# Linear attention with an MLP behind it: one more group with seven block products, and another order of the hand-written steps

## The chip, the cores and the metric

The kernel runs on one core of a Trainium2 chip. The metric is the device time of one launch in microseconds. A core has five engines that run side by side, each with its own queue of instructions, worked off in order: TensorE (PE: matmuls, with PEld for weight loads), VectorE (DVE), ScalarE (ACT), GpSimd (POOL) and SyncE (SP). Here SyncE issues almost all DMAs; the transfers themselves run on 16 DMA engines. An engine's instruction waits on semaphores for what it needs, and everything behind it on that engine waits with it.

## The reference

Inputs are q, k and v of shape (4, 8, 768, 64) (batch, heads, positions, features), a decay `lam` per head, a gain `g_ln` of 512, and two weights of 512 x 2048 and 2048 x 512. The attention is linear, with a decaying state, in blocks of 64 positions:

```
intra = (q_b k_b^T * Dmask) v_b            # Dmask[i,j] = lam^(i-j) for i >= j, else 0
inter = (q_b * lam^(i+1)) state
out_b = intra + inter
state = lam^64 * state + (k_b * lam^(63-i))^T v_b
```

Its output, with the heads side by side, is x of shape (4, 768, 512). Then

```
xn  = (x - mean) / sqrt(var + 1e-6) * g_ln
out = x + relu(xn @ W1) @ W2
```

All inputs and the output are float32.

## The kernel before, in words

**Windows.** The 768 positions of the four batches are cut into 12 windows of 256 positions (`u` = 0 to 11; the batch is `u % 4`). A window's attention yields two tiles of 128 positions, and these two form one *group* of the MLP, also 0 to 11. Windows 0 to 5 and windows 6 to 11 use two forms of the attention; the second has blocks of 64 (`kv64`, `scores64`, `av64`).

**Steps of a window.**
- `open_in` and `load_in` (L87, L92): input tiles `kin`, `qin`, `vin` (three buffers each) and their DMAs on SyncE (L75; from window 6 on two DMAs of 256 KB for each of k, q and v, L79).
- `in_k_one`, `in_q_one`, `in_v` (L240, L245, L251): cast or scale to bf16 in `kq` and `vb`. The engine is an argument: ScalarE, GpSimd or VectorE.
- `transpose_dma` (L266): SyncE issues DMA transposes of k (`a` = 0) and q (`a` = 1) into `kqT`.
- `s1` to `s4` for windows up to 5: `s1` does k-v products (`kv`, L316), the first half's scores (L282), states (L326 on VectorE, L322 on GpSimd) and masks (L292 on VectorE); `s2` the second half's scores and masks; `s3` attention times v (L428) and the first part of the state's share (`inter`, L441) with `seen`, a small read of its result (L452); `s4` the second part, and `norm`: ScalarE copies the result from PSUM to `x` (L463), VectorE takes mean and variance (L465, L466) and writes `xc` (L470).
- `X(u)`, or `X1` and `X2`, for windows from 6 on: the attention's end for window u - 1 (L428 or L415, L441, `norm`) together with the start for window u (L381 k-v products, L362 scores, L397 and L400 states, L368 masks).
- `to_xT` (L486): SyncE issues a DMA transpose of each half of `xc` into `xT`.
- `rstd_of` (L496, L498) and `store` (L698): the factor of the normalization, and the output's DMAs.

**The MLP of a group.** `m1` has 8 units of 8 matmuls of 128 x 256 (L530), each followed by a Relu on ScalarE into `hT` (L533). The second product has two forms, and `WG` (L45) tells from which group on the second is used:
- plain: 8 units of 4 matmuls of 128 x 512 (L666), a tile being finished on VectorE (L690);
- seven block products (`m2w`, `product`, `evict`): hidden blocks are paired, and each pair's 2 x 2 block product with W2 is made with seven products in place of eight, P1 to P7, 8 matmuls of 128 x 256 each (L565), in 8 units of 7. They need sums of hidden blocks (`h_sums`, L548 to L550, VectorE), sums of W2's blocks (`w_sums(c, n)`, L787, L788 and L790, L791, VectorE; four quarters `c`, two halves `n`), and an eviction for each product: L589 and L597 on ScalarE, L590 and L598 on GpSimd, L578 on VectorE.

**PSUM.** A pool `mm` of four banks serves `m1`, both forms of the second product and the k-v products; a new tile waits for the reader of the tile that had its bank. The seven products use all four (`pwa` to `pwd`).

**Order.** Nothing reorders the instructions: the kernel takes manual scheduling, so each engine does its work in the order in which the Python text issues it. The tail of the kernel is a long list of steps, in which `units(n)` takes the next n units of the MLP's plan (group after group, first `m1`, then the second product). A step's place in that list decides its place in the queue of every engine that it uses, SyncE's included.

Of the kernel before, what the change touches and what calls it, by code (L numbers as in the profile page):

```python
# [17 lines left out]
def kernel(  # L18
# [11 lines left out]
    nc = tc.nc  # L30
# [14 lines left out]
    WG = 6  # L45
# [216 lines left out]
    def transpose_dma(u, a):  # L262
        s = st[u]
        if "kqT" not in s:
            s["kqT"] = wk.tile([128, 2, NP, 2, 128], BF16, tag="kqT", bufs=3, name="kqT")
        nc.sync.dma_start_transpose(s["kqT"][:, a].rearrange("p b j t -> p (b j) t"),  # L266
                                    s["kq"][:, a].rearrange("p b j e d -> p (b j e d)"))
# [243 lines left out]
    m2s = {}  # L511
# [184 lines left out]
    def store(u):  # L696
        for j in range(2):
            nc.sync.dma_start(rows_of(u)[j], o_of[u][half[j]])  # L698
# [329 lines left out]
    def units(n):  # L1028
        for _ in range(n):
            f, *a = next(steps)  # L1030
            f(*a)
# [71 lines left out]
    units(2)  # L1103
    rstd_of(3)
    make_keep64()
    units(3)
    store(2)
    transpose_dma(5, 0)
    transpose_dma(5, 1)
    units(1)  # L1110
    s1(4)
    open_in(7, False)
    load_in(7, "k", nc.sync)
    units(1)
    open_window(6)
    in_k_one(6, nc.gpsimd, 0)
    in_k_one(6, nc.gpsimd, 1)
    in_q_one(6, nc.gpsimd, 0)
    in_q_one(6, nc.gpsimd, 1)
    in_v(6, nc.gpsimd)  # L1120
    units(1)
    s2(4)
    units(2)
    s3(4)
    units(2)
    s4(4)
    to_xT(4, 0)
    to_xT(4, 1)
    load_in(7, "q", nc.sync)
    units(2)  # L1130
    transpose_dma(6, 0)
    transpose_dma(6, 1)
    load_in(7, "v", nc.sync)
    units(4)
    s1(5)
    rstd_of(4)
    open_window(7)
# [3 lines left out]
    in_k_one(7, nc.scalar, 1)  # L1141
    units(1)
    s2(5)
    units(3)
    X1(6)
    in_q_one(7, nc.gpsimd, 0)
    in_q_one(7, nc.gpsimd, 1)
    units(1)
    store(3)
    units(1)  # L1150
    transpose_dma(7, 0)
    transpose_dma(7, 1)
    open_in(8, False)
    load_in(8, "k", nc.sync)
    units(2)
    X2(6)
    to_xT(5, 0)
    to_xT(5, 1)
    in_v(7, nc.gpsimd)
# [3 lines left out]
    w_sums(0, 0)  # L1163
    units(1)
    w_sums(0, 1)
    units(1)
    w_sums(1, 0)
    rstd_of(5)
    units(1)
    w_sums(1, 1)  # L1170
    units(4)
    X(7)
    store(4)
    open_in(9, False)
    load_in(9, "k", nc.sync)
    units(1)
    to_xT(6, 0)
    to_xT(6, 1)
    open_window(8)
    in_q_one(8, nc.gpsimd, 0)  # L1180
    in_q_one(8, nc.gpsimd, 1)
    units(1)
    in_k_one(8, nc.scalar, 0)
    units(1)
    in_k_one(8, nc.scalar, 1)
    transpose_dma(8, 0)
    transpose_dma(8, 1)
    load_in(9, "q", nc.sync)
    load_in(9, "v", nc.sync)
    units(2)  # L1190
    in_v(8, nc.gpsimd)
    units(2)
    rstd_of(6)
    units(2)
    w_sums(2, 0)
    units(1)
    w_sums(2, 1)
    units(1)
    w_sums(3, 0)
    units(1)  # L1200
    w_sums(3, 1)
    units(4)
    X(8)
    open_in(10, False)
    load_in(10, "k", nc.sync)
    units(1)
    to_xT(7, 0)
    to_xT(7, 1)
    open_window(9)
    in_q_one(9, nc.gpsimd, 0)  # L1210
    in_q_one(9, nc.gpsimd, 1)
    units(1)
    in_k_one(9, nc.scalar, 0)
    units(1)
    in_k_one(9, nc.scalar, 1)
    transpose_dma(9, 0)
    transpose_dma(9, 1)
    load_in(10, "q", nc.sync)
    load_in(10, "v", nc.sync)
    units(1)  # L1220
    m2s[6].sums(0, 4)
    units(1)
    in_v(9, nc.gpsimd)
    units(2)
    rstd_of(7)
    units(1)
    m2s[6].sums(4, 8)
    units(8)
    X(9)
    open_in(11, False)  # L1230
    load_in(11, "k", nc.sync)
    units(1)
    to_xT(8, 0)
    to_xT(8, 1)
    open_window(10)
    in_q_one(10, nc.gpsimd, 0)
    in_q_one(10, nc.gpsimd, 1)
    units(1)
    in_k_one(10, nc.scalar, 0)
    units(1)  # L1240
    in_k_one(10, nc.scalar, 1)
    transpose_dma(10, 0)
    transpose_dma(10, 1)
    load_in(11, "q", nc.sync)
    load_in(11, "v", nc.sync)
    units(1)
    m2s[7].sums(0, 4)
    units(1)
    in_v(10, nc.gpsimd)
    units(2)  # L1250
    rstd_of(8)
    units(1)
    m2s[7].sums(4, 8)
    units(8)
# [85 lines left out]
```

## Time and profile before

| | before |
|---|---|
| time, median of 5 runs | 213.73 us (211.63 to 215.04) |
| the profiled execution | 213.23 us, with a span of 211.5 us from first to last instruction |
| TensorE busy | 199.8 us (94%) |
| VectorE busy | 142.2 us (67%) |
| ScalarE, GpSimd busy | 97.7 us (46%), 83.0 us (39%) |
| L530, m1's matmuls | 736, 85.0 us |
| L666, plain second product | 192, 43.3 us |
| L548, L549, L550, sums of hidden blocks | 12 each, mean 0.76, 0.60, 0.59 us |

Busy times are from the profile of one execution. Matmuls are pipelined, so that a group's mean length is longer than the distance from one start to the next; where a block of matmuls is priced, starts are subtracted. A wait is put down in the profile to what ended last of what an instruction waits for. The granted TensorE clock is 0.996 of full speed.

### The profile page before, as it was taken

How to read it: one execution, taken by the hardware profiler on the slowest of the kernel's cores; microseconds unless marked ns; L12 is line 12 of the kernel's file. 1: busy time of each engine (PE TensorE's matmuls, PEld its weight loads, DVE VectorE, ACT ScalarE, POOL GpSimd, SP SyncE). 2: the span in 40 equal slices, each digit the busy share in tenths (PEclk: the TensorE clock that was granted, in tenths of full speed). 3: DMA queues.
4: the chain of work that ended last, by engine and by line, in shares of the span. 5: the costliest groups of instructions: out<-in, count | busy, mean ns of one | idle time of the engine just before them, and what ended most of it. 6: DMA issues, size and time to landing. Idle time of an engine off the chain costs nothing.

```text
span 211.5 us, 7148 instructions
## 1 busy us (share of the span) xinstructions
PE 199.8 (94%) x3079; PEld 151.6 (72%) x3079; DVE 142.2 (67%) x293; ACT 97.7 (46%) x195; POOL 83.0 (39%) x113
## 2 busy tenths in 40 slices
PE   2989999999899999999999989999999999999992
PEld 1478788544685576487487478888888888888881
DVE  2577660659267354746997789799797886876253
ACT  3855779120253145246066067185284372661630
POOL 4649039129656083208144155273192202011020
PEclk9999999999999999999999999999999999999998
DMA  4999999999999799999979799997918850430303
GB/s 111 295 271 217 209 287 158 222 299 253 154 334 219 167 224 189 190 183 214 206 170 234 136 212 180 174 213 137 205 31 163 272 141 0 105 52 0 99 16 87
DMA packets 94305, 37.17 MB, mean 176 GB/s; under 512 B 68417, under 2 KB 91457, under 8 KB 94274
## 3 DMA queue, kind: packets, MB, share of 16 engines
q1 hardware_dynamic: 89664, 32.32, 73.8%
q0 software_dynamic: 4224, 4.19, 12.5%
q8 instruction: 24, 0.39, 0.8%
q10 hardware_dynamic: 386, 0.20, 0.4%
q14 instruction: 7, 0.06, 0.1%
HBM read 27.27 MB, written 6.29 MB: 159 GB/s over the span
## 4 chain that ended last, share of the span: by engine, by line
PE 52%; DMA 16%; issue 13%; DVE 9%; POOL 3%; SPq 3%; ACT 1%; POOLq 0%; DVEq 0%; ACTq 0%
PE pm L530 28%; PE pm L666 8%; DMA w<-in_moe_w_ch_dram 4%; DMA qin<-in_q_dram 4%; DMA kin<-in_k_dram 3%; PE pwa L565 3%; DMA xT<-xc 3%; PE pwd L565 2%; PE pwc L565 2%; SPq L75 2%; DMA kqT<-kq 2%; PE po L441 1%; DVE kq L240 1%; DVE wt L790 1%; PE sc L282 1%
## 5 line engine op out<-in xcount | busy, mean ns | idle before, releaser
L530 PE MATMUL pm<-xT,w 128*128 128x256 bf16 x736 | 85.0, 273 | 1.1 <-DMA xT<-xc 1.1
L530 PEld LDWEIGHTS <-w 128*128 128x128 bf16 x736 | 70.0, 98 | 10.7 <-DMA xT<-xc 1.7
L533 ACT ACTIVATE hT<-pm 128x512 f16<-128x512 f32 x92 | 55.2, 602 | 40.9 <-PE pm L530 40.2
L666 PE MATMUL pm<-w,hT 128*128 128x512 f16 x192 | 43.3, 379 | 0.0
L666 PEld LDWEIGHTS <-hT 128*128 128x128 f16 x192 | 18.2, 98 | 20.5
L322 POOL TENSOR_TENSOR Sn<-Stmp,lam_s 128x256 bf16<-128x256 f32 x16 | 9.8, 614 | 50.6 <-DVE Stmp L400 31.9
L565 PEld LDWEIGHTS <-hs 128*128 128x128 f16 x192 | 18.8, 98 | 2.2
L470 DVE SCALAR_TENSOR_TENSOR xc<-po,mv,g_row 128x512 bf16<-128x512 f32 (+1 forms) x24 | 16.8, 705 | 1.8
L292 DVE TENSOR_TENSOR mA<-sc,keep 128x512 bf16<-128x512 f32 x20 | 13.1, 684 | 7.1 <-PE sc L282 7.1
L463 ACT COPY x<-po 128x512 f32<-128x512 f32 x18 | 9.9, 589 | 16.6 <-PE po L441 10.4
L565 PEld LDWEIGHTS <-hT 128*128 128x128 f16 x144 | 13.6, 98 | 2.7 <-ACT hT L533 1.2
L590 POOL TENSOR_TENSOR o<-ev_u,x 128x256 f32<-128x256 f32 x4 | 3.1, 782 | 31.5 <-ACT ev_u L589 31.5
L465 DVE BATCH_NORM_STATS2 stats<-x 128x6 f32<-128x512 f32 x18 | 12.4, 687 | 4.0 <-ACT x L463 3.9
L251 POOL TENSOR_TENSOR vb<-vin,lam_p 128x1024 bf16<-128x1024 f32 x6 | 11.4, 1899 | 6.1 <-DMA vin<-in_v_dram 6.0
L548 DVE TENSOR_TENSOR hs<-hT 128x1024 f16<-128x1024 f16 x12 | 9.1, 762 | 6.8 <-ACT hT L533 6.7
L245 POOL TENSOR_TENSOR kq<-qin,lam_q 128x512 bf16<-128x512 f32 x10 | 10.3, 1046 | 6.9 <-DMA qin<-in_q_dram 6.9
L251 POOL TENSOR_TENSOR vb<-vin,lam_v 128x1024 bf16<-128x1024 f32 (+1 forms) x7 | 11.8, 1687 | 2.7 <-DMA vin<-in_v_dram 1.7
L245 POOL TENSOR_TENSOR kq<-qin,lam_p 128x512 bf16<-128x512 f32 x12 | 12.3, 1044 | 0.7 <-DMA qin<-in_q_dram 0.7
L690 DVE SCALAR_TENSOR_TENSOR o<-pm,rstd,x 128x512 f32<-128x512 f32 x12 | 8.8, 745 | 5.2 <-PE pm L666 5.1
L368 DVE TENSOR_TENSOR mA<-sc,keep 128x512 bf16<-128x512 f32 x12 | 8.2, 683 | 1.6 <-PE sc L362 1.6
L452 ACT COPY seen<-po 128x8 f32<-128x8 f32 x8 | 1.0, 167 | 17.5 <-PE po L441 17.5
L441 PE MATMUL po<-Sn,kqT 64*64 64x64 bf16 x216 | 7.5, 198 | 0.3 <-DVE seen L452 0.3
(139 smaller groups left out, 267.7 us busy)
## 6 DMA issues: line engine op xcount, KB each, us to landing
out_dram<-o SPq DMA_DIRECT2D x18, 256.0 KB, 4.9
w<-in_moe_w_ch_dram POOLq DMA_DIRECT2D x8, 512.0 KB, 9.1
kin<-in_k_dram SPq DMA_DIRECT2D x14, 256.0 KB, 4.7
qin<-in_q_dram SPq DMA_DIRECT2D x14, 256.0 KB, 4.7
vin<-in_v_dram SPq DMA_DIRECT2D x14, 256.0 KB, 5.3
kin<-in_k_dram SPq DMA_DIRECT2D x5, 512.0 KB, 7.1
qin<-in_q_dram SPq DMA_DIRECT2D x5, 512.0 KB, 8.8
vin<-in_v_dram SPq DMA_DIRECT2D x5, 512.0 KB, 8.4
```

Source lines behind the costliest of these rows:

```text
L245: eng.tensor_tensor(part(1, st[u]["kq"], ALL)[:, :, :, j], src[:, :, :, j], lq[:, :, :, None].to_broadcast([128, NP, 2, D]), op=ALU.mult)
L251: eng.tensor_tensor(st[u]["vb"][:, hs], qkv_in[u]["v"][:, hs], lv.to_broadcast([128, n, 2, D]), op=ALU.mult)
L292: nc.vector.tensor_tensor(s[f"mA{hf}"][:, e], s[f"sc{hf}"][e], kp[:, None, :, :].to_broadcast([128, 2, 2, 128]), op=ALU.mult)
L322: eng.tensor_tensor(dst, src, lam_s[:, :, None].to_broadcast([128, NP, D]), op=ALU.mult)
L441: nc.tensor.matmul(s["po"][ab][half[jq], 2 * p + e, :], lhsT=qT[half[e], p, jq, half[ab]], rhs=s["S"][ab][jq][half[e], p, :], start=False, ...
L463: nc.scalar.copy(x, po)
L465: nc.vector.bn_stats(stats, po if early else x)
L470: nc.vector.scalar_tensor_tensor(xc[:, sl], in0=po[:, sl], scalar=mv[:, 0:1], in1=g_row[:, sl], op0=ALU.subtract, op1=ALU.mult)
L530: nc.tensor.matmul(pm[:, b, :], lhsT=w1[n // W2K][:, kk, (n % W2K) * 128:(n % W2K + 1) * 128], rhs=xT_of[g][:, kk, 0:N], start=(b == 0 and ...
L533: nc.scalar.activation(hT[:, u * NB:(u + 1) * NB, 0:N], pm, ACT.Relu)
L565: nc.tensor.matmul(pr[bank], lhsT=lhs(r), rhs=rhs, start=(first and r == 0), stop=(r == KB // 2 - 1), skip_group_check=True)
L666: nc.tensor.matmul(acc[i], lhsT=hT[:, kk, i * 128:(i + 1) * 128], rhs=w2[kk // W2K][:, kk % W2K, :], start=(kk == 0), stop=(kk == KB - 1))
```

## The change: what it does

`WG` goes from 6 to 5, so group 5 takes the seven products too. The sums of W2 are issued during groups 3 and 4 in place of groups 4 and 5, and the sums of group 5's hidden blocks (`m2s[5].sums`) are added. The steps of windows 4 to 11 between group 2's second product and group 8 stand in another order; some are cut up, and some casts and scalings change their engine. The list up to group 2 and from X(10) on is the same. In the diff, lines that both lists have in the same place are left out in part.

```diff
...
-    WG = 6
+    WG = 5
...
     load_in(6, "q", nc.sync)
     units(1)
     load_in(6, "v", nc.sync)
-    units(2)
+    units(1)
+    transpose_dma(5, 0)
+    units(1)
     rstd_of(3)
     make_keep64()
-    units(3)
-    store(2)
-    transpose_dma(5, 0)
     transpose_dma(5, 1)
-    units(1)
-    s1(4)
     open_in(7, False)
     load_in(7, "k", nc.sync)
     units(1)
+    s1(4)
     open_window(6)
-    in_k_one(6, nc.gpsimd, 0)
+    in_k_one(6, nc.scalar, 0)
+    units(1)
     in_k_one(6, nc.gpsimd, 1)
-    in_q_one(6, nc.gpsimd, 0)
-    in_q_one(6, nc.gpsimd, 1)
+    units(2)
+    open_window(7)
+    s2(4)
+    store(2)
+    units(2)
+    w_sums(0, 0)
+    w_sums(0, 1)
+    s3(4)
+    units(1)
+    w_sums(1, 0)
+    in_q_one(6, nc.vector, 1)
     in_v(6, nc.gpsimd)
-    units(1)
-    s2(4)
-    units(2)
-    s3(4)
-    units(2)
     s4(4)
+    in_q_one(6, nc.vector, 0)
+    units(3)
+    load_in(7, "q", nc.sync)
     to_xT(4, 0)
     to_xT(4, 1)
-    load_in(7, "q", nc.sync)
-    units(2)
+    units(1)
+    w_sums(2, 0)
+    units(1)
+    open_in(8, False)
+    units(1)
+    s1(5)
+    units(1)
+    transpose_dma(6, 1)
+    units(1)
+    rstd_of(4)
+    in_q_one(7, nc.gpsimd, 0)
+    units(1)
+    in_q_one(7, nc.gpsimd, 1)
+    s2(5)
     transpose_dma(6, 0)
-    transpose_dma(6, 1)
-    load_in(7, "v", nc.sync)
-    units(4)
-    s1(5)
-    rstd_of(4)
-    open_window(7)
-    units(1)
-    in_k_one(7, nc.scalar, 0)
-    units(1)
-    in_k_one(7, nc.scalar, 1)
-    units(1)
-    s2(5)
     units(3)
     X1(6)
-    in_q_one(7, nc.gpsimd, 0)
-    in_q_one(7, nc.gpsimd, 1)
-    units(1)
+    in_k_one(7, nc.vector, 1)
+    load_in(7, "v", nc.sync)
     store(3)
-    units(1)
+    load_in(8, "k", nc.sync)
+    in_v(7, nc.gpsimd)
+    units(1)
+    in_k_one(7, nc.scalar, 0)
+    units(1)
+    open_window(8)
+    units(2)
+    X2(6)
+    units(2)
+    w_sums(1, 1)
+    to_xT(5, 0)
     transpose_dma(7, 0)
     transpose_dma(7, 1)
-    open_in(8, False)
-    load_in(8, "k", nc.sync)
-    units(2)
-    X2(6)
-    to_xT(5, 0)
+    units(1)
+    open_in(9, False)
+    in_k_one(8, nc.vector, 1)
+    units(1)
+    in_k_one(8, nc.gpsimd, 0)
+    units(2)
     to_xT(5, 1)
-    in_v(7, nc.gpsimd)
+    units(1)
+    w_sums(3, 0)
+    units(1)
+    rstd_of(5)
+    w_sums(3, 1)
+    units(1)
+    w_sums(2, 1)
     load_in(8, "q", nc.sync)
     load_in(8, "v", nc.sync)
     units(2)
-    w_sums(0, 0)
-    units(1)
-    w_sums(0, 1)
-    units(1)
-    w_sums(1, 0)
-    rstd_of(5)
-    units(1)
-    w_sums(1, 1)
-    units(4)
     X(7)
-    store(4)
-    open_in(9, False)
-    load_in(9, "k", nc.sync)
-    units(1)
-    to_xT(6, 0)
-    to_xT(6, 1)
-    open_window(8)
+    units(1)
     in_q_one(8, nc.gpsimd, 0)
     in_q_one(8, nc.gpsimd, 1)
-    units(1)
-    in_k_one(8, nc.scalar, 0)
-    units(1)
-    in_k_one(8, nc.scalar, 1)
+    load_in(9, "k", nc.sync)
+    units(1)
+    in_v(8, nc.gpsimd)
+    units(1)
+    to_xT(6, 0)
+    transpose_dma(8, 1)
     transpose_dma(8, 0)
-    transpose_dma(8, 1)
+    to_xT(6, 1)
     load_in(9, "q", nc.sync)
     load_in(9, "v", nc.sync)
-    units(2)
-    in_v(8, nc.gpsimd)
-    units(2)
-    rstd_of(6)
-    units(2)
-    w_sums(2, 0)
-    units(1)
-    w_sums(2, 1)
-    units(1)
-    w_sums(3, 0)
-    units(1)
-    w_sums(3, 1)
-    units(4)
-    X(8)
     open_in(10, False)
     load_in(10, "k", nc.sync)
+    units(3)
+    m2s[5].sums(0, 4)
+    units(2)
+    store(4)
+    load_in(10, "v", nc.sync)
+    units(2)
+    open_window(9)
+    units(1)
+    m2s[5].sums(4, 8)
+    units(3)
+    in_k_one(9, nc.scalar, 0)
+    units(1)
+    in_k_one(9, nc.scalar, 1)
+    units(1)
+    in_q_one(9, nc.gpsimd, 0)
+    X(8)
+    units(1)
+    in_q_one(9, nc.gpsimd, 1)
+    open_window(10)
+    units(3)
+    open_in(11, False)
     units(1)
     to_xT(7, 0)
+    units(1)
+    rstd_of(7)
+    transpose_dma(9, 1)
+    transpose_dma(9, 0)
     to_xT(7, 1)
-    open_window(9)
-    in_q_one(9, nc.gpsimd, 0)
-    in_q_one(9, nc.gpsimd, 1)
-    units(1)
-    in_k_one(9, nc.scalar, 0)
-    units(1)
-    in_k_one(9, nc.scalar, 1)
-    transpose_dma(9, 0)
-    transpose_dma(9, 1)
+    rstd_of(6)
+    units(4)
+    m2s[6].sums(0, 4)
+    m2s[6].sums(4, 8)
+    units(3)
     load_in(10, "q", nc.sync)
-    load_in(10, "v", nc.sync)
-    units(1)
-    m2s[6].sums(0, 4)
-    units(1)
+    units(4)
     in_v(9, nc.gpsimd)
-    units(2)
-    rstd_of(7)
-    units(1)
-    m2s[6].sums(4, 8)
-    units(8)
+    in_k_one(10, nc.gpsimd, 1)
+    in_k_one(10, nc.gpsimd, 0)
     X(9)
-    open_in(11, False)
+    in_v(10, nc.gpsimd)
+    in_q_one(10, nc.gpsimd, 0)
+    units(1)
+    transpose_dma(10, 0)
+    units(1)
+    rstd_of(8)
+    in_q_one(10, nc.vector, 1)
+    units(1)
+    to_xT(8, 0)
+    units(2)
+    to_xT(8, 1)
+    units(1)
+    transpose_dma(10, 1)
+    units(3)
+    m2s[7].sums(0, 4)
+    m2s[7].sums(4, 8)
+    units(1)
+    load_in(11, "q", nc.sync)
+    units(1)
     load_in(11, "k", nc.sync)
-    units(1)
-    to_xT(8, 0)
-    to_xT(8, 1)
-    open_window(10)
-    in_q_one(10, nc.gpsimd, 0)
-    in_q_one(10, nc.gpsimd, 1)
-    units(1)
-    in_k_one(10, nc.scalar, 0)
-    units(1)
-    in_k_one(10, nc.scalar, 1)
-    transpose_dma(10, 0)
-    transpose_dma(10, 1)
-    load_in(11, "q", nc.sync)
+    units(2)
     load_in(11, "v", nc.sync)
-    units(1)
-    m2s[7].sums(0, 4)
-    units(1)
-    in_v(10, nc.gpsimd)
-    units(2)
-    rstd_of(8)
-    units(1)
-    m2s[7].sums(4, 8)
-    units(8)
+    units(3)
     X(10)
     units(1)
     to_xT(9, 0)
```

## The prediction, made before the run

> **What bounds the kernel now.** I read the page first: shares, then slices. Each digit of the slices is a tenth busy in a fortieth of the span (5.3 us).
>
> ```profile
> PE 199.8 (94%) x3079; PEld 151.6 (72%) x3079; DVE 142.2 (67%) x293; ACT 97.7 (46%) x195; POOL 83.0 (39%) x113
> ...
> PE   2989999999899999999999989999999999999992
> ...
> DVE  2577660659267354746997789799797886876253
> ...
> DMA  4999999999999799999979799997918850430303
> ```
>
> TensorE is full from slice 3 to 39, so a microsecond of matmul taken out there is a microsecond of time, and every new TensorE wait is paid in full. But the DMA engines are full too, up to slice 28 (148 us), and VectorE runs at eight tenths in the second half: two more resources with little to spare in the stretch that is reordered (69 to 150 us). Next the TensorE timeline, which has start, length, work and, in brackets, the idle time before and what ended it:
>
> ```profile
> 72.02 1.03 PE L530 MATMUL pm<-xT,w 128*128 128x256 bf16 x8 [0.25 <-DMA xT<-xc]
> ...
> 75.44 0.70 PE L282 MATMUL sc<-kqT 64*64 64x128 bf16 x16
> ...
> 105.52 0.45 PE L415 MATMUL po<-vb,mA 64*64 64x64 bf16 x32
> ...
> 106.98 0.19 PE L441 MATMUL po<-Sn,kqT 64*64 64x64 bf16 x1 [0.28 <-DVE seen L452]
> ...
> 107.30 7.18 PE L530 MATMUL pm<-xT,w 128*128 128x256 bf16 x64
> 114.32 7.07 PE L666 MATMUL pm<-w,hT 128*128 128x512 f16 x32
> ...
> 122.87 0.44 PE L362 MATMUL sc<-kqT 64*64 64x64 bf16 x32 [0.72 <-DMA kqT<-kq]
> ```
>
> These are all the waits of TensorE in the stretch: 0.25 us for group 3's xT, 0.28 us inside the scores of window 4 (15 of the 16 matmuls start only at 75.72, when the second mask of the first half is done), 0.28 us for VectorE's `seen`, 0.72 us for window 8's kqT. Together 1.53 us. Lastly the shares of the DMA engines over stretches of one or two groups (a share over 1 is transfers that overlap on the engines' rings):
>
> ```profile
> 72.00:89.70 17.70, 17.64 (x320) 11.48 (x320) 10.38 (x22) 7.19 (x13) 7.48 (x9) 1.00 1.24 204
> 89.70:107.30 17.60, 17.32 (x392) 12.04 (x385) 12.90 (x31) 6.01 (x11) 5.77 (x7) 1.00 1.14 194
> 107.30:123.40 16.10, 15.38 (x227) 10.46 (x218) 12.62 (x26) 7.03 (x15) 6.02 (x8) 1.00 0.87 187
> ```
>
> The last two columns are DMA share and GB/s. Up to 107 us the DMA engines have no slack: what is put ahead of a transfer in SyncE's order delays it by its own length.
>
> **What the Trainium skill says.** "TensorE: Matmul & The Clock Gate", Back-to-back issue gap, gives 262 cycles for 256 columns and 518 for 512 at 2.4 GHz, so about 109 and 216 ns. The trace agrees: 64 L530 matmuls take 7.09 us on the chain (111 ns), 32 L666 take 7.00 us from start to start (219 ns). "DMA: Bandwidth & Descriptors", Issuing engines are not separate DMA queues, says all issues run on the same 16 engines; here landings follow SyncE's order about 1.2 us per 256 KB load. "SBUF — State Buffer", Who interferes with whom, says a VectorE operation with two SBUF inputs, or a copy in a two-port mode, and a GpSimd operation that reads SBUF exclude each other for a whole instruction. The trace shows it: one L790 took 2.08 us, against 0.42, from 115.31 on, beside GpSimd's 1.90 us L251 that began at 115.21.
>
> **The change, part by part.** The sum is against the profiled execution, 213.23 us with 211.5 us of span; the median of the runs is 0.5 us above it.
>
> *Products of group 5.* Out go 32 L666 matmuls: 7.00 us. In come 56 L565: group 6's took 130.53 to 136.74, 6.21 us. TensorE: -0.79 us.
>
> *VectorE and the others in group 5.* VectorE loses two L690 (1.5 us) and gains six L548 to L550 (0.76+0.60+0.59, twice: 3.9 us) and six L578 (3.1 us), net +5.5 us; ScalarE gains two 0.47 us evictions, GpSimd two of 0.75 us. Four quarters of W2's sums only move. This work lies beside the matmuls, costing nothing as long as VectorE is not late for a bank, and I follow that below. `seen` of window 6 moves from VectorE to ScalarE (the test `u > WG`), which is idle there: the 0.28 us wait goes.
>
> *First half of window 4 (s1) three units of 0.88 earlier.* kv(4) now ends at about 70.2 us, but window 4's second kqT transpose, whose place in SyncE's queue is unchanged, landed at 70.70 us: new wait 0.55. What is queued behind it on TensorE is everything, so it is paid in full. In exchange group 3's xT (PE at 72.02) has a block more in front of it and is there: -0.25. s2(4) now comes three units after s1(4), so both masks are done: -0.28.
>
> *Window 6's preparation, taken from GpSimd.* Its first k half is now cast on ScalarE and waits there for k(6), landed at 74.1; behind it stands the Relu of group 3's first m1 tile, ready at 73.7, done by 75.4, and its bank is wanted again at 77.8: 0. Both q halves (L245; on VectorE some 0.7 us each, from L292's 0.68 for the same 512 columns; 2.6 if GpSimd's L251 locks one out) and seven pairs of W2's sums stand among VectorE's steps of windows 4 and 5. The tightest is the first: four sums of 1.6 us between the masks, over at 75.65, and `seen` of window 4, which is done at about 77.5; TensorE wants it at 77.6. A lock-out would delay xc(4) from 80.6 to 82.5 at most, still before SyncE gets to it. 0 (0 to 0.4).
>
> *Window 5's transposes before store(2).* They landed at 83.4 and 85.8; without the two stores (2 to 2.5 us) ahead, about 83.4 for the second. The scores of s1(5), now three units earlier, want it at 83.5 to 83.8. I take 0.1 (0 to 0.4).
>
> *Window 7's q loads ahead of group 4's xT.* This is the largest item. Landings are from the DMAs' semaphores in the trace. Before, the last xT landed at 89.05 and the matmuls wanted it at 89.73. Now two q loads of 1.2 to 1.5 us stand ahead: landing 91.5 to 92.1. The matmuls come later as well, by X1(6) in front of them (1.07 us) and the net of the waits above (0.12), so at 90.9. Wait 0.6 to 1.2; I take 0.9.
>
> *Window 6's transposes after it.* The set of transfers up to them is the old one, so they land at 95.57 as before. X2(6) wants them at 91.82 + 4 x 0.886 = 95.4. Wait 0.2.
>
> *Casts of windows 7 and 8 onto VectorE, window 8's k load ahead of window 7's transposes.* k(8) landed at 105.41; two transposes (2.0 us) fewer ahead make it 103.4. VectorE's L240 for window 8 waits for that, and behind it in VectorE's order stand half of the sums for W2's quarter 3, L690, a reciprocal, the other half, and the second half of quarter 2: 0.5+0.76+0.75+0.07+0.85+0.85 = 3.8 us, to 107.2. Then X(7)'s states: L397, L400, a mask, L397, 1.9 us with GpSimd's L322 beside the mask, to 109.1. That last one frees the bank of group 5's second m1 tile, which TensorE wants at 95.57 + 0.51 (X2) + 4 x 0.886 + 7 x 0.875 + 1.24 (X) + 0.875 + 0.886 = 108.8. Wait 0.3.
>
> *Window 7's and 8's transposes.* Window 7's land by 106.5 (same set as up to xT5 before, 106.52), wanted at about 106.5: 0. Window 8's q products are on GpSimd by 111.3, landing 3.3 us after issue, some 5 us before X(8): -0.72.
>
> *X(8) inside the last product, P3.* Its second kv bank waits for P6's two evictions (VectorE near 121.3 by the same counting, TensorE at 121.2), 0.1; P3's own eviction queues behind X(8)'s norm and frees the seventh m1 tile of group 6 at about 128.4 against 128.3: 0.1. Later steps of groups 6 to 8 (the sums of hidden blocks late; window 9's v and window 10's k on GpSimd behind the additions L590 and L598; SyncE's window 11 loads after window 10's transposes) leave 0.1 to 1 us of cover each by the same counting: 0 (0 to 0.8).
>
> Sum: saved 0.79+0.25+0.28+0.28+0.72 = 2.32; paid 0.55+0.1+0.9+0.2+0.3+0.2 = 2.25. Net -0.1: 213.1 for the profiled execution, 213.6 at the median.
>
> **The rivals.**
> 1. *Covered.* Transfers regroup so that xT and k(8) are in time, and only the certain 0.55 us is paid: 213.7 - 2.32 + 0.55 = 212.0. For it: rings interleave, so landing order is not strictly issue order. Against: shares of 1.24 and 1.14.
> 2. *Slower: VectorE held by its cast of k(8).* If that load lands where it did before (105.4), the bank is free at 111.1 instead of 109.1, so 2.05 us more: 215.7; a cast locked out by GpSimd's other half of the same k (L240 on VectorE ranged from 0.41 to 2.12 us) adds up to 1.6. I take 216.3. From k(8) later than 103.1 us on, each microsecond is one of time. For it: VectorE already has 12.9 of 17.6 us in that stretch and takes 5.5 us more soon after. Against: the two transposes really are behind it now.
> 3. That the products don't come out as meant can't be: 56 for 32 matmuls stand in TensorE's order.
>
> **How the numbers follow.** Forecast 0.50, own range 212.7 to 214.8 (its items' ends, and the slack of 0.1 us in three places). Covered 0.20, slower 0.30. Low end 211.8, below rival 1 by the spread of the runs; high end 216.6, so that only the worse part of the locked-out cast is left out. About 1% (2.1 us) is what a measurement tells here from no change. Faster by more than that needs nearly all of rival 1: 0.12. Slower by over 1%, past 215.9: most of rival 2 and a little of the forecast: 0.28. Same: 0.60.
>
> **What would show it.** Right: group 5's m2 6.2 us; waits of TensorE of some 0.5 us before window 4's scores and 0.5 to 1.2 us before group 4's first m1 on DMA xT; none before X(8)'s scores; a short one on VectorE's L397 in group 5. Wrong: no xT wait (rival 1), VectorE idle over 3 us before L240 (rival 2), or waits in groups 6 to 8, where I have none.

## The result, and the profile after

| | before | after |
|---|---|---|
| median of all executions | 212.69 us (80, 211.23 to 215.56) | 215.26 us (43, 212.88 to 218.68) |
| median without the slow ones | 212.53 us (71) | 214.50 us (28) |
| ratio, after to before, of these | | 1.0103, 95% interval 1.0085 to 1.0121 |
| profiled execution, span | 213.23 us, 211.5 us | 215.51 us, 213.8 us |
| TensorE, VectorE busy | 199.8, 142.2 us | 199.5, 146.6 us |

Here and below, an execution that took over 1.5 % more than the fastest of its kernel counts as slow and is left out of the medians and ratios of runs. The forecast was "no change" (213.6 us); measured is slower by 1.0 %. How much of that is the change's, the controls below tell. The slices of the page of after:

```profile
PE 199.5 (93%) x3103; PEld 154.3 (72%) x3103; DVE 146.6 (69%) x306; ACT 96.7 (45%) x195; POOL 82.8 (39%) x114
...
PE   2988699999999999898999998999999999999992
...
DVE  2586571448556688746879877789798896876253
...
DMA  4999999999999999999998799896969960430403
```

A slice is 5.3 us. In the reordered stretch TensorE now falls below 9 tenths in slices 17, 19 and 25 (from 85.5, 96.2 and 128.3 us on); before it did so in slice 24 alone. In the start, whose instructions are the same, slices 4 and 5 are emptier too. The timeline of the reordered stretch, with idle time before an instruction and its cause in brackets:

```profile
72.29 0.42 PE L282 MATMUL sc<-kqT 64*64 64x128 bf16 x16 [0.38 <-DMA kqT<-kq]
...
86.12 0.42 PE L282 MATMUL sc<-kqT 64*64 64x128 bf16 x16 [0.80 <-DMA kqT<-kq]
...
93.44 3.70 PE L530 MATMUL pm<-xT,w 128*128 128x256 bf16 x32
...
97.74 0.45 PE L362 MATMUL sc<-kqT 64*64 64x64 bf16 x32 [0.61 <-DMA kqT<-kq]
...
117.14 1.14 PE L565 MATMUL pwa<-w,hT 128*128 128x256 f16 x8
...
122.48 0.27 PE L565 MATMUL pwd<-w,hs 128*128 128x256 f16 x1
```

The first six products of group 5 take 122.48 - 117.14 = 5.34 us for 48 matmuls, so 6.23 us for 56: the 0.79 us are there. New are three waits for transposes of k and q (before the scores of windows 4, 5 and 6). Group 4's first m1 (93.44) waits for nothing here. A fourth wait, for P3's eviction behind window 8's norm, is in the list of waits:

```profile
PE sc L282 <- DMA kqT<-kq: 1.2, 2, 0.8
PE pm L530 <- DVE o L578: 0.7, 1, 0.7
PE sc L362 <- DMA kqT<-kq: 0.6, 1, 0.6
```

The columns are us in total, times, longest. The prediction gave rival 1 the sign "no xT wait". The sign is here, and the rival is not: the kernel is slower. The stretches of groups 3, 4 and 5, in the columns that the prediction showed:

```profile
74.38:93.44 19.06, 18.26 (x386) 12.09 (x384) 14.71 (x32) 6.35 (x12) 5.87 (x7) 1.00 1.23 197
93.44:110.05 16.61, 16.00 (x277) 10.94 (x274) 11.74 (x28) 7.29 (x16) 4.63 (x7) 1.00 1.06 195
110.05:124.70 14.65, 14.65 (x242) 12.70 (x240) 12.96 (x25) 7.98 (x17) 7.72 (x10) 1.00 0.92 183
```

Blocks of attention have moved from one group to another, so the sum counts: 50.3 us, against 51.4 before. Yet group 3 starts at 74.38 us in place of 72.02. From the start of group 2 (56.77, before 55.28) to that of group 3 it is 0.9 us more, since the first half of window 4 now stands in it, and the first 55 to 57 us, in which both kernels have the same instructions, are 1.5 us longer. From group 2's start to group 6's the two traces differ by 0.2 us only (67.9 and 68.1). So one trace of each tells little, and the experiments had to separate the start from the rest.

### The profile page after: what moved, and what is told of

It reads as the page before. It is cut to its first block, busy times and chain, and to the rows that moved or that the text cites. A ratio compares the mean times of both kernels' runs of the same rounds, so it can differ in the third digit from the quotient of the medians.

```text
span 213.8 us, 7214 instructions
## 1 busy us (share of the span) xinstructions
PE 199.5 (93%) x3103; PEld 154.3 (72%) x3103; DVE 146.6 (69%) x306; ACT 96.7 (45%) x195; POOL 82.8 (39%) x114
## 4 chain that ended last, share of the span: by engine, by line
PE 51%; issue 14%; DMA 13%; SPq 8%; DVE 7%; POOL 3%; ACT 1%; POOLq 0%; DVEq 0%; ACTq 0%
PE pm L530 23%; PE pm L666 10%; DMA vin<-in_v_dram 7%; DMA kqT<-kq 4%; PE pwa L565 4%; SPq L75 3%; PE pwc L565 3%; SPq L79 2%; PE pwd L565 2%; DVE xc L470 2%; PE pwb L565 2%; SPq L266 2%; DMA xT<-xc 2%; DVE stats L465 1%; DVE kq L240 1%
## 5 line engine op out<-in xcount | busy, mean ns | idle before, releaser
L533 ACT ACTIVATE hT<-pm 128x512 f16<-128x512 f32 x92 | 54.5, 601 | 43.7 <-PE pm L530 43.1
L666 PE MATMUL pm<-w,hT 128*128 128x512 f16 x160 | 36.8, 380 | 0.0
L666 PEld LDWEIGHTS <-hT 128*128 128x128 f16 x160 | 14.9, 98 | 16.5
L565 PEld LDWEIGHTS <-hs 128*128 128x128 f16 x224 | 21.9, 98 | 2.5
L322 POOL TENSOR_TENSOR Sn<-Stmp,lam_s 128x256 bf16<-128x256 f32 x16 | 9.8, 617 | 31.9 <-DVE Stmp L400 17.1
L565 PEld LDWEIGHTS <-hT 128*128 128x128 f16 x168 | 15.9, 98 | 3.2 <-ACT hT L533 1.4
L590 POOL TENSOR_TENSOR o<-ev_u,x 128x256 f32<-128x256 f32 x5 | 4.2, 844 | 33.1 <-ACT ev_u L589 33.1
L548 DVE TENSOR_TENSOR hs<-hT 128x1024 f16<-128x1024 f16 x14 | 11.1, 791 | 7.6 <-ACT hT L533 7.6
L245 POOL TENSOR_TENSOR kq<-qin,lam_q 128x512 bf16<-128x512 f32 x10 | 10.3, 1046 | 9.5 <-DMA qin<-in_q_dram 9.5
L245 POOL TENSOR_TENSOR kq<-qin,lam_p 128x512 bf16<-128x512 f32 x9 | 9.3, 1045 | 6.1 <-DMA qin<-in_q_dram 3.1
L550 DVE TENSOR_TENSOR hs<-hs,hT 128x512 f16<-128x512 f16 x14 | 8.8, 628 | 0.5
L690 DVE SCALAR_TENSOR_TENSOR o<-pm,rstd,x 128x512 f32<-128x512 f32 x10 | 7.4, 745 | 2.2 <-PE pm L666 2.2
```

The source lines that it names most:

```text
L245: eng.tensor_tensor(part(1, st[u]["kq"], ALL)[:, :, :, j], src[:, :, :, j], lq[:, :, :, None].to_broadcast([128, NP, 2, D]), op=ALU.mult)
L322: eng.tensor_tensor(dst, src, lam_s[:, :, None].to_broadcast([128, NP, D]), op=ALU.mult)
L533: nc.scalar.activation(hT[:, u * NB:(u + 1) * NB, 0:N], pm, ACT.Relu)
L548: nc.vector.tensor_tensor(s13, b[:, :, 1:2, :].to_broadcast([128, n, 2, 128]), b[:, :, 0:4:3, :], op=ALU.subtract)
L565: nc.tensor.matmul(pr[bank], lhsT=lhs(r), rhs=rhs, start=(first and r == 0), stop=(r == KB // 2 - 1), skip_group_check=True)
L666: nc.tensor.matmul(acc[i], lhsT=hT[:, kk, i * 128:(i + 1) * 128], rhs=w2[kk // W2K][:, kk % W2K, :], start=(kk == 0), stop=(kk == KB - 1))
```

## The experiments

**How the traces are compared.** Two quantities: *T*, from group 2's first m1 to the last instruction, which leaves the unchanged start out; and *W*, the sum of TensorE's waits in it, each taken as the distance between two matmul starts less the usual distance on that line (so a little larger than the idle time in brackets), from 0.15 us up. Six traces had a mean granted clock of 0.984 to 0.992 (e0b_after, e1_products, e6b_q7, e7_q7_both, e13_x1_later, e14_x1_one); from them only single waits are used.

| | group 2 at | *T* | *W* | 154.5 + *W*, less 0.8 with the products |
|---|---|---|---|---|
| before | 55.28 | 156.25 | 2.02 | 156.5 |
| c_before, c2_before, c3_before | 56.14, 54.52, 54.76 | 155.31, 155.27, 156.24 | 0.92, 0.78, 1.80 | 155.4, 155.3, 156.3 |
| after, e0_after, e0c_after | 56.77, 54.77, 54.88 | 157.00, 157.75, 156.66 | 3.13, 3.89, 2.99 | 156.8, 157.6, 156.7 |
| e2_order | 55.24 | 156.96 | 2.37 | 156.9 |
| e5_both | 56.21 | 156.04 | 2.58 | 156.3 |
| e6_q7 | 56.65 | 155.45 | 1.79 | 155.5 |
| e8_spread, e8b_spread | 56.53, 54.59 | 154.82, 155.17 | 1.39, 1.51 | 155.1, 155.2 |
| e10_q7_ahead | 56.09 | 157.27 | 3.06 | 157.5 |
| e16_x1_unit | 56.24 | 157.11 | 3.29 | 157.0 |

The constant 154.5 is c2_before's *T* less its *W*; one constant and the products' 0.8 us (0.79) give every *T* within 0.3 us. What the kernels differ by, past the start, is therefore the products and TensorE's waits. Means of *T*: 155.77 us for four traces of before, 157.14 for three of after, +1.37 us. Means of *W*: 1.38 and 3.34 us, so 1.96 us more of waits, of which the products give back 0.79.

**The changed kernel again, and its two halves.** e0_after is the changed kernel. e2_order has the new order with the plain product in group 5. e1_products has before's order with the seven products there, the sums of its hidden blocks, and W2's sums a group sooner; against before:

```diff
-    WG = 6
+    WG = 5
...
-    units(4)
+    w_sums(0, 0)
+    units(1)
+    w_sums(0, 1)
...
     s1(5)
...
-    units(2)
-    w_sums(2, 0)
...
+    m2s[5].sums(4, 8)
```

and e2_order, against after:

```diff
-    WG = 5
+    WG = 6
...
-    m2s[5].sums(0, 4)
...
-    m2s[5].sums(4, 8)
```

> The changed kernel again, for a second profile and an interval on the same chip as the others. Theory 1 (the loss is the four waits of TensorE in the reordered stretch, and the 1.5 us by which the unchanged start ran later in the first profile is chance of the loads): ratio to before 1.002 to 1.006, the start (up to the last L441 of window 3) anywhere between 65.3 and 67 us. Theory 2 (the start is later because of the change, though its instructions are the same): ratio 1.010 again, start at 66.8 us again.

> The order of before, with the seven products in group 5, W2's sums one group sooner and the hidden blocks' sums of group 5 where group 6 has them. Theory 1: faster than before by the 0.79 us of matmuls, less what VectorE's added 5.5 us delays: ratio 0.996 to 1.000, group 5's second product 6.2 us long. Theory 2 makes no start of its own here, so the same. Rival, VectorE becomes late with the products alone: a wait of TensorE on VectorE over 0.5 us in groups 4 or 5, ratio 1.001 to 1.006.

> The order of after, with group 5's second product left in the plain form (its sums of hidden blocks left out). Theory 1: the waits on the three kqT transposes stay (0.4, 0.8, 0.6 us) and the gain of 0.79 us is gone: ratio 1.005 to 1.010, slower than the changed kernel by 0 to 0.4 per cent. Theory 2 (start): ratio 1.012 or more with a start near 66.8 us.

Measured ratios: 1.0065 (1.0027 to 1.0102), 1.0108 (1.0039 to 1.0177) and 1.0100 (1.0062 to 1.0139); medians 214.07, 214.90 and 214.78 us (9, 5 and 10 executions). Both halves alone came out at least as slow as the whole, so the two are no sum, and the ratios do not tell the theories apart. The traces do. Theory 2 is out: window 3's last L441 starts at 64.80 us in e0_after, where after had 66.81 and before 65.31. e1_products waits where W2's sums stand in front of window 5's masks on VectorE (1.13 and 0.58 us) and for hidden sums (0.94); e2_order where the order puts it (0.68 and 0.37 us before windows 4 and 5's scores, 1.05 before window 6's). So the products have a cost of their own when W2's sums stand badly. e0_after showed the wait that the first trace lacked:

```profile
89.85 0.71 PE L428 MATMUL po<-vb,mA 64*64 64x64 bf16 x64
...
93.66 1.59 PE L530 MATMUL pm<-xT,w 128*128 128x256 bf16 x13 [2.52 <-DMA xT<-xc]
```

**The matmul steps later.** e5_both, against after (`s1(4)` and `X2(6)` one unit later, `s1(5)` two, `s2(5)` one, `X(8)` behind the last product unit), DMAs in the same order:

```diff
-    s1(4)
     open_window(6)
...
     units(1)
+    s1(4)
...
+    units(1)
     X(8)
-    units(1)
```

> The changed kernel with the four waiting steps put later: the first half of window 4 and X2 of window 6 one unit, the first half of window 5 two units and its second half one, and X(8) behind the last unit of group 5's products. SyncE's order is unchanged. Theory 1: the waits of 0.38, 0.80, 0.61 and 0.65 us of TensorE go: 2.4 us faster than the changed kernel, ratio to before 0.990 to 0.996. Theory 2: at most the 0.7 us of the stretch comes back, ratio 1.005 to 1.008 with a start near 66.8 us.

Measured 1.0105 (1.004 to 1.017, 6 executions), median 214.87 us. *T* fell to 156.04 us, since the waits for kqT before windows 4, 5 and 6 are gone or below 0.2 us. It did not fall further, because others came: 0.55 us on a mask, 0.41 on xT, 0.49 on window 7's kqT, so that *W* is still 2.58 us. The ratio did not fall at all. That a kernel with *T* below that of the one trace of before (156.25) should be 1 % slower put the comparison itself in question.

**The control.** c_before, c2_before and c3_before are the kernel before, unchanged, timed in the place of a changed one, beside another copy of itself.

> The kernel before itself, built and timed as if it were a changed one: a control for the comparison and a second trace of the same program. Theory 1 (the 2 us are lost between groups 2 and 6, by waits that the new order of the DMAs makes): ratio 1.000 within 0.003, group 2's first m1 anywhere between 54.5 and 58 us of the span, and from there to the end 156.0 to 156.5 us. Theory 2 (the changed kernels begin their second group later, by some 1 to 1.5 us, although the instructions up to there are the same): group 2's first m1 here at 54.5 to 55.5 us, where the changed kernels had 54.8 to 58.0. If the comparison itself favours the kernel before: ratio about 1.008.

> The kernel before itself again, second in the call where the first control was first. Theory 3: ratio 1.005 to 1.011 again. If the first control was an accident of that one build or of its place in the call: ratio 0.997 to 1.003.

> The kernel before a third time, as the control of this call. From group 2's first m1 to the end 155.2 to 156.3 us; ratio to the comparison's own copy anywhere between 0.994 and 1.010, if copies of one program differ as the first two controls did (1.0083 and 0.9958).

Measured: 1.0083 (1.0058 to 1.0108), 0.9958 (0.9931 to 0.9984), 0.9962 (0.9936 to 0.9987); the second lies outside both ranges expected for it. The same program differs from itself by up to 0.8 %, with intervals that exclude 1: these hold the scatter of executions, not that between one loaded copy of a program and the next. Medians of the three copies are 213.83, 212.31 and 212.83 us; those of the copies that stood beside as before, 212.53, 212.32, 212.05, 213.46, 213.60 and 213.73. Different chips are not the reason, or not alone: 212.05 and 213.83 us were measured together on one chip, 213.46 and 212.31 on another. Mean of the nine: 213.0 us.

The changed kernel was measured four times too: ratios 1.0103, 1.0065, 1.0018 (0.9995 to 1.0041) and 1.0033 (0.9983 to 1.0084), medians 214.50, 214.07, 213.90 and 214.54 us, mean 214.25. Two of the four intervals include 1. So the change costs about 1.3 us (0.6 %) by the medians and 1.4 us by *T*: slower, by little more than half of the 1.0 % of the result. The rest of the 1.0 % is which copies met. One trace of each control suggests where copies differ: group 2 begins at 56.14 us in the one with 213.83 us, at 54.52 and 54.76 in those with 212.31 and 212.83. Whether that is a property of the copy or of the one execution that was traced, and what makes the same start longer, was not tried.

**The move of window 7's q loads.** e6_q7 and e6b_q7 take it out of the changed kernel; e7_q7_both does that with e5_both's edits; e10_q7_ahead makes that one move in the kernel before:

```diff
 e10_q7_ahead, against before
+    load_in(7, "q", nc.sync)
     to_xT(4, 0)
     to_xT(4, 1)
-    load_in(7, "q", nc.sync)
```

> The changed kernel with one move undone: window 7's two q loads go back behind group 4's xT transposes on SyncE. Theory 1: the wait on DMA xT before group 4's first m1 goes, group 4 begins 1 to 2 us sooner than the 93.4 and 93.7 us of the two traces of the changed kernel, and the median falls by 0.7 to 1.5 us, ratio 0.999 to 1.004. Theory 2: ratio within 0.003 of the changed kernel's 1.0065 to 1.0103, whatever becomes of that wait.

> The changed kernel with that move undone and with the matmul steps of windows 4 to 6 and 8 put later as well (first halves of windows 4 and 5, second half of window 5, window 6's second part, window 8's step behind the last product unit). Theory 1: every wait of 0.4 us or more between groups 3 and 6 is gone, the products' 0.79 us are left, and the kernel is as fast as the kernel before or up to 1 us faster: ratio 0.996 to 1.001. Theory 2: ratio 1.005 to 1.010.

> The kernel before with one move of the change alone: window 7's two q loads go ahead of group 4's xT transposes on SyncE. Against the control of this call. By the prediction's step: a wait on DMA xT before group 4's first m1 of 0.6 to 1.2 us beyond what is there, median 0.5 to 1.2 us above the control. By the trace that had the longest such wait: 2.7 us of it, median 2 to 2.7 us above. If the transposes keep their time whatever stands ahead: no wait, within 0.3 us of the control.

> The changed kernel once more, to be set against the second control of this call and not against the comparison's own copy of the kernel before. Theory 3 (most of the measured 1.0 % belongs to the comparison, since the kernel before itself came out 0.8 % above its own copy; the change costs 0.3 to 1.2 us): ratio to the copy 1.007 to 1.013, median 0.3 to 1.2 us above the control's of this call. Theory 1 in full (the change costs 2 us): 1.7 to 2.5 us above the control.

> The changed kernel with window 7's q loads behind group 4's xT, once more, since its first run had few executions. Its first trace: no wait on xT, 155.45 us from group 2's first m1 to the end. If that move and what it collides with are the main loss: again no wait on xT, 155.2 to 155.9 us there, and a median within 0.4 us of the control of this call.

e10_q7_ahead, e0b_after and c2_before were timed together. Medians: 213.72, 213.90 and 212.31 us (13, 19 and 22 executions). One move alone made the kernel before 1.4 us slower (1.5 us by *T*), nearly as much as the whole change did there (1.6 us, which lies between the ranges of both theories). Its trace has a wait on xT, 1.39 us idle, 1.59 from start to start, both above the 0.6 to 1.2 expected:

```profile
90.34 0.42 PE L282 MATMUL sc<-kqT 64*64 64x128 bf16 x16
92.14 2.79 PE L530 MATMUL pm<-xT,w 128*128 128x256 bf16 x24 [1.39 <-DMA xT<-xc]
```

and SyncE's timeline (start, length of the issues, queue) shows why: it never pauses, and each issue pushes the next.

```profile
82.93 2.06 SPq L79 DMA_DIRECT2D kin<-in_k_dram  x2
85.03 2.00 SPq L79 DMA_DIRECT2D qin<-in_q_dram  x2
87.12 3.25 SPq L486 DMA_TRANSPOSE xT<-xc  x2
```

e6_q7 has no wait on xT and a *T* of 155.45 us, 1.7 below the changed kernel's mean. Its ratio (1.0116, 4 executions) says nothing beside a control at 1.0083; its median is 0.6 us above that control's (214.41 to 213.83). e7_q7_both: 213.99 us, 1.0077 (1.0051 to 1.0104), 0.2 above the control, though in a trace with 2.35 us of xT wait before group 7 and 0.92 us before window 9's scores. The expectation for it, no wait of 0.4 us or more between groups 3 and 6, failed as well (0.53 on a mask, 0.88 on L397). e6b_q7: 213.95 us beside a control of 212.83, so 1.1 us more where I expected at most 0.4. Its trace has no wait on xT, but 2.74 us on window 6's states, and VectorE's and GpSimd's timelines tell the chain:

```profile
95.96 0.42 DVE L397 TENSOR_TENSOR Smid<-pk,Sn 128x256 f32<-128x256 f32 x1 [3.82 <-POOL Sn L322]
```

```profile
94.31 1.04 POOL L245 TENSOR_TENSOR kq<-qin,lam_p 128x512 bf16<-128x512 f32 x1 [0.79 <-DMA qin<-in_q_dram]
95.31 0.61 POOL L322 TENSOR_TENSOR Sn<-Stmp,lam_s 128x256 bf16<-128x256 f32 x1
```

In the new order window 7's scaling of q (L245) stands ahead of window 6's state (L322) in GpSimd's queue. With the q loads late, GpSimd waits for them, VectorE for GpSimd, and a bank of m1 for VectorE. So this move was not undone by itself without a new loss: early q loads hold up xT, late ones the states (0.61 us in e6_q7, 2.74 in e6b_q7).

**What made xT 2.7 us late.** The q loads explain 1.6 us where nothing stands in front as cover (e10_q7_ahead). In e0_after and e0b_after the wait was 2.70 and 2.62 us although 112 small matmuls of window 6's first part (about 1.1 us) stood in front of it as cover. The DMA view of e0_after for 90.6 to 93.8 us, in slices of 0.08 us:

```profile
DMA  9999739000000599999999970012001000999999
...
q1 hardware_dynamic: 1410, 0.35, 95.4%
q8 instruction: 1, 0.02, 2.9%
```

The digits are busy tenths; q1 and q8 are the queues of SyncE's DMAs and of instructions. The engines are not full here: idle from 91.2 to 91.6 and nearly so from 92.6 to 93.3 us. In between is one packet of 16 KB of an instruction queue, at 91.11 us; some 20 packets of 256 bytes that start behind it, at 92.1 to 92.5 us (the second transpose, by their place), end only by 93.4. In e0b_after the packet is at 93.32 us and the matmuls start at 95.96; in after it comes at 93.79, once xT is there, and in e0c_after at 90.77, just as it lands. In these two it falls just in front of or among the packets of window 6's first transpose instead, which lands 4.9 and 4.6 us after its issue. To move the packet, I moved the small matmuls that TensorE runs through when it comes: two m1 units later in e13_x1_later, one in e14_x1_one and e16_x1_unit.

```diff
 e16_x1_unit, against after
-    units(3)
+    units(4)
     X1(6)
...
     in_v(7, nc.gpsimd)
-    units(1)
     in_k_one(7, nc.scalar, 0)
```

> The changed kernel with window 6's first part (64 x 64 matmuls of window 5's end and window 6's k-v products) two m1 units later; window 7's q loads stay ahead of group 4's xT. Theory 4 (two of three traces of the changed kernel have group 4's xT held up by 2.1 us more than the q loads explain, because a 16 KB packet of the instruction queue, fetched as TensorE runs through the 112 small matmuls in front of group 4's first m1, meets the second transpose on the DMA engines): the packet now comes after that landing, the second xT lands within 0.7 us of the first, and group 4's first m1 waits 0.8 to 1.8 us, with its start at 91.3 to 92.5 us in place of 93.4 to 93.7. If the transposes are slow for the order of SyncE's DMAs alone: the second half lands 2 us or more after the first, a wait of 3 us or more, start still at 93.4 or later. Median 0.3 to 1 us below the changed kernel's 214.0 to 215.4 by theory 4, no less otherwise.

> The same with one unit in place of two. Theory 4: as there, group 4's first m1 at 91.3 to 92.5 us after a wait of 0.8 to 1.8 us. Otherwise: start at 93.4 or later.

> The changed kernel with window 6's first part one m1 unit later, everything that follows it in the list still behind it (the two kernels before this one had let it slip behind GpSimd's scaling of v(7), which waits for a load until 97 to 101 us, so that window 6's states waited on GpSimd). Theory 4: second xT within 0.7 us of the first, group 4's first m1 waits 1.0 to 1.8 us, none of 1 us or more on L397, and from group 2's first m1 to the end 155.9 to 156.9 us where the changed kernel had 157.0 and 157.75; median 0.3 to 1.5 us below the changed kernel's of this call. If the order of the DMAs alone makes the wait: as the changed kernel.

> The changed kernel as it is, a fourth trace. Theory 4: if the 16 KB packet that comes as TensorE runs through window 6's first part falls ahead of the second xT's landing, a wait of 2 to 2.8 us before group 4's first m1; if it falls behind, 0 to 0.6 us there. From group 2's first m1 to the end 156.8 to 158 us at full clock.

The packet moved with them (97.02, 94.12, 95.81 us), and in all three the second transpose landed some 0.6 us after the first, with waits of 1.15, 1.61 and 1.97 us, the last above its range. Group 4's first m1 starts at 90.98 us in e14_x1_one and at 94.20 in e13_x1_later, whose group 2 began only at 58.32. e16_x1_unit for the same window of time:

```profile
DMA  9999932200168999999410000004999999999999
...
q1 hardware_dynamic: 1740, 0.43, 77.6%
...
xT<-xc SPq DMA_TRANSPOSE x1
```

No packet, and m1 begins at 92.75 us. So the 2.6 to 2.7 us go with the packet's place: of all traces with the q loads ahead, only the two in which a packet comes just in front of the second transpose's own packets have them. The later packet brought no time: it now meets window 6's second transpose, which lands 5.1 us after its issue; m1 asks for xT 1.1 us sooner; and *T* of e16_x1_unit is 157.11 us, where I expected 155.9 to 156.9; its median, 213.96 us, is 0.6 below that of the changed kernel beside it (214.54, 7 executions). e0c_after had 0.43 us on xT, as expected for a packet that comes late, and *T* 156.66, just under the range given. e13_x1_later and e14_x1_one were far slower (218.28 us, and 218.76 in two executions), which no theory had: my edit had let window 6's part slip behind `in_v(7)` on GpSimd. GpSimd's timeline of e14_x1_one:

```profile
97.82 1.90 POOL L251 TENSOR_TENSOR vb<-vin,lam_p 128x1024 bf16<-128x1024 f32 x1 [6.62 <-DMA vin<-in_v_dram]
99.67 0.61 POOL L322 TENSOR_TENSOR Sn<-Stmp,lam_s 128x256 bf16<-128x256 f32 x1
```

GpSimd waits 6.6 us for v(7) with window 6's state behind it, and m1 then 4.0 us for its bank in e14_x1_one, 2.9 in e13_x1_later.

The 20 traces bear it out. Of the transposes of k and q issued after 56 us, take those whose issue took under 1.35 us and whose landing is in the trace. With no packet of queue 8 starting between 0.5 us after the issue and 0.5 us before the landing, 106 of them landed 3.28 us after their issue (median; nine of ten within 3.4). With one, 61 landed after 4.61 us (eight of ten from 4.2 to 5.0). That is so in the kernel before as well, as with window 6's second transpose (4.68 us), from which the prediction took its landing of 95.57 us.

**The products without the order.** e8_spread and e8b_spread keep before's DMAs and steps, and put W2's sums where VectorE stood idle and window 8's v behind the hidden sums:

```diff
-    WG = 6
+    WG = 5
...
     s3(4)
-    units(2)
+    units(1)
+    w_sums(0, 0)
+    units(1)
+    w_sums(0, 1)
     s4(4)
...
     s2(5)
-    units(3)
+    units(1)
+    w_sums(1, 0)
+    units(1)
+    w_sums(1, 1)
+    units(1)
     X1(6)
...
+    m2s[5].sums(0, 4)
+    units(3)
+    rstd_of(6)
+    m2s[5].sums(4, 8)
+    units(1)
     in_v(8, nc.gpsimd)
```

> The kernel before with its own order, group 5 with seven block products, and W2's sums put where VectorE stands idle in the trace of before (two pairs between the attention and the norm of window 4, two after the second half of window 5, four where it had four), and window 8's v scaled behind group 5's hidden sums. No DMA is moved. Theory 1: no new wait above 0.3 us in groups 3 to 6, so the products' 0.79 us and the wait for seen (0.28 us) are gained: median 0.5 to 1.1 us below before, ratio 0.995 to 0.998. Theory 2: ratio 1.003 to 1.010 as in the other kernels with the products.

> The kernel before in its own order of DMAs, with the products of group 5 and W2's sums in VectorE's idle stretches, once more, against the control of this call. Theory 3: median 0.3 to 1.1 us below the control, ratio to the copy 1.002 to 1.006. If the products bring nothing: within 0.2 us of the control.

Medians 213.48 us (7 executions; control 213.83) and 212.15 (21; control 212.31): 0.35 and 0.16 us less, where I expected 0.3 to 1.1. With controls that differ by 1.5 us among themselves, that is no difference. *T* is 154.82 and 155.17, some 0.8 us below the mean of before, but with new waits of 0.37 us on L397 and 0.5 us on window 8's kqT that use up part of the gain. e8b_spread is 1.7 us faster than the changed kernel beside it (213.90), and not measurably faster than the kernel before.

## Why the prediction was wrong

By its own steps, against *T*: forecast 156.25 - 0.1 = 156.15 us, measured 157.14 (mean of after, e0_after, e0c_after), 0.99 more. The waits that it forecast sum to 2.25 us; measured are 3.34, from start to start. (By the idle times in brackets, about 0.2 us less for each, they are 2.70.)

| step | forecast | after, e0, e0c | mean less forecast |
|---|---|---|---|
| s1 of window 4 three units earlier | 0.55 | 0.56, 0.57, under 0.15 | -0.17 |
| window 5's transposes before store(2) | 0.1 | 0.99, 0.62, 0.61 | +0.64 |
| window 7's q loads ahead of group 4's xT | 0.9 | none, 2.70, 0.43 | +0.14 |
| window 6's transposes after it | 0.2 | 0.77, none, 1.08 | +0.42 |
| VectorE's cast of k(8) | 0.3 | none | -0.30 |
| X(8) inside P3; group 5's hidden sums in e0c | 0.2 | 0.81, none, 0.87 | +0.36 |

- **Right.** The products' 0.79 us. The waits for group 3's xT, for window 4's mask, for `seen` and for window 8's kqT went, with no trace of after showing one. VectorE's cast of k(8) did no harm: it stood idle 0.4 to 1.1 us before it, where rival 2's sign was over 3. So the direction of rival 2, slower, came true for another reason.
- **The step that failed** is "Window 5's transposes before store(2)": "without the two stores (2 to 2.5 us) ahead, about 83.4 for the second. [...] I take 0.1 (0 to 0.4)". It measured 0.61 to 0.99 us (0.57 in e0b_after), the largest excess in either way of measuring, and in every trace. The wait stands where I looked for one, the landing was wrong: I took the stores' whole length off it. SyncE's timelines of c2_before and e0_after, and TensorE's of e0_after:

```profile
76.97 3.88 SPq L266 DMA_TRANSPOSE kqT<-kq  x2
```

```profile
75.67 4.81 SPq L266 DMA_TRANSPOSE kqT<-kq  x2
...
83.76 0.42 PE L282 MATMUL sc<-kqT 64*64 64x128 bf16 x16 [0.44 <-DMA kqT<-kq]
```

SyncE comes to these transposes 1.3 us earlier, but issuing them takes 0.9 us longer, and the second landed at 84.33 us in c2_before, by 83.76 in e0_after. It is so in all traces, counted from group 2's start. Eight have the old order here, ten have the new one with the scores waiting. SyncE comes to the pair 2.2 us earlier in the new order (mean), as the stores' length says; the pair lands only about 1.5 us earlier, at 28.4 to 29.4 us in place of 29.8 to 30.5. I had counted on 2.4 us and 28.1. The last load of window 6 lands at nearly the same time in both orders (24.7 to 25.5 and 25.2 to 25.8 us), so the transposes now come to a queue in which these loads still stand. A second cause fits as well: an instruction packet falls into this pair in every trace of either order, and in 14 of the 18 the pair lands 2.9 to 3.3 us after that packet begins. No run parts the two, so what sets this landing stays open.
- "Window 6's transposes after it" assumed that an unchanged set of transfers ahead means an unchanged landing (95.57, which is 40.3 us from group 2's start). It was 40.6 us in e0c_after, 40.9 in after and 41.6 in e0_after, where TensorE was late itself and did not wait. In after and e0c_after the packet falls on the first of the pair: the second landed 5.7 us after the first's issue, in e10_q7_ahead, with no packet near, after 4.5. The difference, about 1.2 us, is enough for the two waits (0.77 and 1.08).
- "Window 7's q loads": the landing was reckoned well where no packet falls in between (36.2 to 36.8 us from group 2's start; m1 starts at 36.0 in e0c_after and e10_q7_ahead, 36.5 in e16_x1_unit), and 1.6 us or more too early in the two traces where one does (38.9 and 38.4). That the mean of the waits (1.04 us) comes near 0.9 is luck: of none, 2.70, 2.62 and 0.43 us none lies in the range of 0.6 to 1.2. Nothing in my working looked at the packet. The expectation for e10_q7_ahead took that range over unworked: with no X1(6) in front of m1, my own landing gives 1.8 to 2.4 us there, and 1.59 were measured.
- "Up to 107 us the DMA engines have no slack: what is put ahead of a transfer in SyncE's order delays it by its own length" was read from mean shares over 17 us (1.24, 1.14). Over 19 us of after the share is as high (1.23); in e0_after and e16_x1_unit the slices above show idle stretches of 0.4 to 0.7 us around transposes within it.
- **The base was one trace.** The profile of before has a *T* of 156.25 us, 0.48 above the mean of four. Of the 2.32 us that I counted as saved, the 0.72 us of window 8's kqT are in none of the three controls, and group 3's xT (0.25 us) was a wait in one of them alone (0.32). So even the items that came true saved less than they seemed to. The 1.37 us of *T* are these parts: -0.1 forecast, 0.99 by which after exceeds the forecast, 0.48 by which the base was too high.

The measured median, 215.26 us, lies in the range given (211.8 to 216.6); the forecast of no change does not hold. What stays open: what sets the landing of window 5's transposes, why copies of one program differ by up to 0.8 %, and why a transpose beside a 16 KB instruction packet takes 1.3 us more, or 2.

## What to carry to other kernels

Where SyncE issues DMAs without a pause, as here, a transfer's landing cannot be had by subtracting the lengths of what was taken from in front of it: 2.4 us taken off gave 1.5. Look at what it waited for, and price a step that wants it within 1 us of its landing as a wait. Steps that move earlier on one engine move against every queue that feeds them: q loads, GpSimd's scaling and window 6's states formed one chain, in which early loads held up one transfer and late loads another engine. Before a 1 % difference is explained, run the unchanged kernel in the changed one's place, and compare traces from a common event on, not from the start.

## What was not expected of the hardware

- Instructions come by DMA while the kernel runs: queue 8, of kind "instruction", has 24 packets of 16 KB (0.39 MB) in e0_after. The Trainium skill, "Runtime: NRT & Kernel Launch", Instruction fetch mechanics, says that the sequencer fetches blocks of 16 KiB (256 instructions) by a DMA queue of its own and that the cost is mostly hidden. The size agrees. By an estimate from that page, 64 bytes an instruction, the 3103 matmuls of TensorE and as many weight loads are 6206 x 64 bytes = 0.397 MB, so the queue is taken for TensorE's. Hidden it was not for the DMA transposes: one with such a packet beside it landed 1.3 us later in the median of 20 traces, before's among them, and xT some 2 us later in two of four traces of the changed kernel. That it goes with the packet's place is shown, its cause is not.
- The Trainium skill, "DMA: Bandwidth & Descriptors", Queues, rings and completion order, has one candidate for it: a semaphore's increment lands only after every earlier write of that DMA engine, across its queues. No run here tells that from packets simply held up.
- Copies of one program had medians from 212.1 to 213.8 us, each with a scatter of single executions of about 3 to 5 us.
